# A fused attention and gated feed-forward kernel: the first half of the input weight loaded and converted in pieces of 256 columns, in a new order of the first operations

## The chip, the cores and the metric

One Trainium2 chip, one of its cores. The metric is the device time of one execution in microseconds (us), the median of the runs shown. Engines: PE (matmuls), DVE (vector), ACT (scalar), POOL (GpSimd), and SP, whose queue issues every DMA of this kernel.

## What is computed

```python
# chunked attention: 24 chunks of 32 queries, each with 16 keys to the left, 8 to the right and 8 memory keys
scores = scale * q_c @ k_full.T ; a = softmax(scores)
out[:, :, chunk] = a @ v_full            # B=4, 8 heads, 768 places, 64 wide
# gated feed-forward over x = attention output, 512 wide; moe_w_in 512x1024, moe_w_out 1024x512
h = maximum(x @ w_in, 0)
conv_out = sum over k of conv_w[k] * h shifted by k - 1 places, k = 0, 1, 2
return (h * sigmoid(conv_out)) @ w_out
```

The weights `w_in`, `conv_w` and `w_out` come in double precision, as 64-bit words; `q`, `k`, `v` and the memory are single precision.

## The kernel before

**A list of operations and an order written out by hand.** The function makes 1,818 operations; each names its engine, what it reads and what it writes. `ORDER` then says in which order they are issued. Every engine works through its own operations strictly in that order, and an operation waits until what it reads is there and until its buffer is free. The DMAs are all issued from SP's queue, in the same order.

**Attention** (`attention`, 32 steps, one for each batch, half of the sequence and pair of heads). A step n loads Q (384 KB), K (252 KB) and V (384 KB); PE makes the scores (24 small matmuls, L427, called S n here); DVE takes the row maximum (L436), ACT the exponential, DVE the row sum (L474) and its reciprocal (L476); DVE or POOL normalizes (L479); PE transposes (three matmuls, L491, T n), ACT places the result in two copies (L498); PE multiplies by V (24 small matmuls, L540, V n); ACT copies the high part of the result x (L546), and DVE makes the low part (L550). A value is held as a high and a low part, and a product of two such values is three matmuls.

**Weights** (`from_f64`). A part of `w_in` is 128 rows by 512 columns, 512 KB as 64-bit words. It is loaded into one of four `w64` buffers; ACT takes the magnitude (L306), DVE, ACT and POOL put the high and the low part together in some ten operations. The letter in `W_IN` says in which way: N (5 operations on DVE, and 4 matmuls on PE with an ACT copy behind them, L355 to L360), M (7 on DVE), S (5 on DVE, 2 on POOL), C (6 on DVE, 1 on POOL). Two `w_top` buffers hold the intermediate values, so at most two parts are in work at a time.

**Feed-forward in** (`ffn_in`). For a batch, a block fc of 128 of the 1,024 inner columns and a half hf of the sequence, PE sums over four cc (three 384-column matmuls each, L577; called a product here, fc/cc). Block fc of 0 to 3 takes columns 128 fc to 128 fc + 127 of the parts 0 to 3, one part for each cc; block fc of 4 to 7 takes the whole part fc. So before the change the first product needs all 512 columns of part 0, converted, and both parts of x from step 0; four blocks of the accumulators (`f`) are open at a time.

Then come `gated` (the convolution, the gate and the split into parts, on ACT and DVE), and the second matrix product (L793, or for batches 1 to 3 a seven-product scheme, L736).

Of the kernel before, what the change touches and what calls it, by code (L numbers as in the profile page):

```python
# [29 lines left out]
W_IN, W_OUT, W_CONV = "NMMSCMMM", "CmMMMMMC", "s"  # L30
# [193 lines left out]
def attention_then_gated_ffn(  # L224
# [68 lines left out]
    def from_f64(src, hi, lo, key, n, kind):  # L293
# [7 lines left out]
        def op(eng, cost, do, r, wr, **kw):  # L301
            plan.op(eng, cost, do, r, wr, **kw)
# [638 lines left out]
```

## Time before, and how its profile is read

| | us |
|---|---|
| median of 3 runs | 336.43 (336.32 to 336.48) |
| the profiled execution, its own time | 337.24 |
| its span, first to last instruction | 335.5 |
| PE busy in the span | 322.1 (96%) |
| DVE busy | 296.4 (88%) |
| ACT busy | 222.6 (66%) |
| POOL busy | 51.2 (15%) |

Times in the views count from the span's start. Matmuls are pipelined, so a matmul's duration covers part of the next one's; the distance from start to start says what it costs. The same holds for DVE: an instruction's duration can reach into the next.

### The profile page before, as it was taken

What the parts mean: (1) busy time and instruction counts of PE and PEld (TensorE: products, weight loads), DVE (VectorE), ACT (ScalarE), POOL (GpSimd) and SP (SyncE); (2) the same over time, 40 slices, a digit from 0 to 9 for tenths busy, and PEclk for the clock granted to TensorE, in tenths of its full rate; (3) what the DMA queues carried; (4) which work ended last, traced back from release to release, by engine and by line L of the source; (5) the groups of instructions that cost most, each with busy time, mean ns of one, the idle gap of its engine ahead of it and who ended that gap; (6) DMA issues with size and microseconds to landing.
All of it is one profiled execution on the core that took longest, in us unless ns stands there. A gap on an engine that the chain in (4) does not pass through costs nothing.

```text
span 335.5 us, 8308 instructions
## 1 busy us (share of the span) xinstructions
PE 322.1 (96%) x3259; PEld 305.1 (91%) x3259; DVE 296.4 (88%) x516; ACT 222.6 (66%) x502; POOL 51.2 (15%) x72
## 2 busy tenths in 40 slices
PE   0899999999999999999999999999999999999995
PEld 0689999999999999899988878999999999999995
DVE  3998998999999989899999999999999999599311
ACT  3588896887787879759787527658886486355210
POOL 2150310302104010410020312000000600700000
PEclk9999999999999999999999999999999999999999
DMA  8999998699697969650412545131032642011013
GB/s 278 401 372 345 388 342 291 218 300 293 202 328 230 295 193 342 218 167 34 129 61 80 195 134 198 75 146 47 2 109 64 195 135 96 26 56 63 33 65 110
DMA packets 31144, 60.87 MB, mean 181 GB/s; under 512 B 3584, under 2 KB 18048, under 8 KB 31104
## 3 DMA queue, kind: packets, MB, share of 16 engines
q1 hardware_dynamic: 31104, 60.33, 53.3%
q8 instruction: 26, 0.43, 0.5%
q14 instruction: 14, 0.11, 0.1%
HBM read 47.93 MB, written 12.39 MB: 180 GB/s over the span
## 4 chain that ended last, share of the span: by engine, by line
PE 89%; DMA 5%; DVE 2%; ACT 2%; issue 1%; SPq 0%; ACTq 0%
PE f L577 38%; PE f L736 15%; PE f L793 10%; PE s L736 7%; PE ta L540 7%; PE s L427 6%; PE ta L736 4%; DMA w<-in_w_out_dram 2%; PE ta L491 2%; DMA out_dram<-k 1%; DMA w<-in_w_in_dram 1%; ACT e L462 1%; ACT w_top L306 0%; PE f L355 0%; DVE w_top L323 0%
## 5 line engine op out<-in xcount | busy, mean ns | idle before, releaser
L577 PE MATMUL f<-u,w_in_hi 128*128 128x384 f32 x512 | 140.8, 343 | 0.6 <-ACT u L587 0.6
L577 PEld LDWEIGHTS f<-u,w_in_hi 128*128 128x128 f32 x512 | 93.2, 188 | 2.7 <-ACT u L587 1.1
L577 PE MATMUL f<-u,w_in_lo 128*128 128x384 f32 x256 | 86.0, 336 | 0.0
L607 DVE SCALAR_TENSOR_TENSOR u<-u,cw,u 128x767 f32<-128x767 f32 x64 | 64.4, 1027 | 0.1
L577 PEld LDWEIGHTS f<-u,w_in_lo 128*128 128x128 f32 x256 | 48.2, 188 | 0.2
L644 DVE TENSOR_TENSOR u<-u,u 128x768 fp32r<-128x768 f32 (+1 forms) x55 | 46.5, 871 | 0.8 <-ACT u L641 0.8
L641 ACT CAST u<-u 128x768 fp32r<-128x768 f32 (+1 forms) x56 | 41.1, 765 | 8.3 <-PE s L736 2.8
L736 PE MATMUL f<-w_in_hi,u 128*128 128x256 f32 x216 | 45.0, 282 | 0.0
L587 ACT ACTIVATE u<-f 128x384 f32<-128x384 f32 x64 | 30.6, 490 | 15.9 <-PE f L577 15.0
L736 PEld LDWEIGHTS f<-w_in_hi,u 128*128 128x128 f32 x216 | 36.0, 188 | 0.0
L616 DVE SCALAR_TENSOR_TENSOR u<-u,u 128x768 f32<-128x768 f32 x32 | 31.4, 993 | 0.4 <-ACT u L611 0.4
L793 PE MATMUL f<-w_out_hi,u 128*128 128x512 f32 x96 | 31.6, 397 | 0.0
L462 ACT ACTIVATE e<-s,top 128x64 f32<-128x64 f32 x132 | 29.3, 324 | 3.4 <-DVE w L509 1.6
L611 ACT ACTIVATE u<-u 128x768 f32<-128x768 f32 x32 | 26.8, 847 | 6.1 <-DVE u L607 6.0
L736 PE MATMUL f<-w_in_lo,u 128*128 128x256 f32 x108 | 30.3, 281 | 0.0
L598 ACT ACTIVATE u<-u,cw 128x768 f32<-128x768 f32 x30 | 28.3, 944 | 2.7 <-DVE z L476 1.3
L479 POOL TENSOR_TENSOR e<-e,z 128x384 f32<-128x384 f32 x22 | 20.6, 936 | 54.1 <-DVE z L476 35.3
L753 ACT COPY w<-f 128x256 f32<-128x256 f32 x18 | 6.6, 374 | 27.3 <-PE f L736 22.8
L427 PE MATMUL s<-k,u 128*64 128x64 f32 x672 | 24.7, 224 | 0.0
L427 PEld LDWEIGHTS s<-k,u 128*64 128x64 f32 x672 | 21.8, 138 | 3.1 <-issue 2.2
L759 DVE TENSOR_TENSOR k<-s,w 128x256 f32<-128x256 f32 x18 | 7.6, 422 | 17.1 <-PE s L736 9.6
L651 POOL TENSOR_TENSOR u<-u,u 128x384 f32<-128x384 f32 x9 | 10.8, 1200 | 74.6 <-DVE u L616 62.0
(99 smaller groups left out, 609.6 us busy)
## 6 DMA issues: line engine op xcount, KB each, us to landing
u<-in_q_dram SPq DMA_DIRECT2D x32, 384.0 KB, 6.2
u<-in_v_dram SPq DMA_DIRECT2D x25, 384.0 KB, 5.4
k<-in_k_dram SPq DMA_DIRECT2D x28, 252.0 KB, 4.9
out_dram<-k SPq DMA_DIRECT2D x36, 128.0 KB, 1.7
w<-in_w_in_dram SPq DMA_DIRECT2D x8, 512.0 KB, 6.7
w<-in_w_out_dram SPq DMA_DIRECT2D x8, 512.0 KB, 5.9
y_dram<-u SPq DMA_DIRECT2D x8, 384.0 KB, 2.8
u<-y_dram SPq DMA_DIRECT2D x8, 384.0 KB, 3.4
```

Source lines behind the costliest of these rows:

```text
L427: nc.tensor.matmul(s.t[j * D : (j + 1) * D, o : o + KW], lhsT=q_[:, c], rhs=k_t.t[:, c * STEP : c * STEP + KW], start=True, stop=True,)
L462: A.activation(keys(e)[:, g // 2, g % 2], s_()[:, g // 2, g % 2], AF.Exp, bias=top.t[:, g : g + 1], scale=SCALE)
L577: nc.tensor.matmul(f.t[:, :TW], lhsT=w_in_p[c][:, part, col : col + P], rhs=x.t[:, a * TW : (a + 1) * TW], start=(cc == 0 and i == 0), sto ...
L587: "A", act(TW, True), lambda: A.activation(h.t[:, hf * TW : (hf + 1) * TW], f.t[:, :TW], AF.Relu, scale=0.5), (f,), ((h, hf),)
L598: plan.op("A", act(S, ptr=1), lambda: A.activation(c.t, h.t, AF.Copy, scale=w[1]), H, (c,))
L607: lambda j=j, to=to, at=at: V.scalar_tensor_tensor(out=c.t[:, to], in0=h.t[:, at], scalar=w[j], in1=c.t[:, to], op0=ALU.mult, op1=ALU.add) ...
L611: plan.op("A", act(S), lambda: A.activation(c.t, c.t, AF.Tanh), (c,), (c,), table="exp")
L616: lambda: V.scalar_tensor_tensor(out=y.t, in0=c.t, scalar=1.0, in1=h.t, op0=ALU.add, op1=ALU.mult),
L641: plan.op("A", act(n), lambda: A.copy(out=hi(), in_=src()), (y,), (k_hi,))
L644: lambda: (V if eng == "V" else G).tensor_tensor(out=low(), in0=src(), in1=hi().bitcast(F32), op=ALU.subtract),
L736: nc.tensor.matmul(ps.t[:, :n], lhsT=l[a](), rhs=w[c], start=(first and j == 0 and m == 0), stop=(j == hf - 1 and m == 2), skip_group_chec ...
L793: nc.tensor.matmul(ps.t[:, :n], lhsT=gs[b, fc][a].t[:, tt * P : (tt + 1) * P], rhs=w_out_p[c][:, fc, o : o + n], start=(fc == 0 and i == 0 ...
```

## The change

The parts 0 to 3 of `w_in` are each loaded and converted in two pieces of 256 columns (called 0a, 0b, and so on), each with a key of its own, so that a product waits for its piece alone: blocks fc 0 and 1 for the a pieces, blocks 2 and 3 for the b pieces. The ways of conversion stay with the parts (0: N, 1 and 2: M, 3: S, 4: C, 5 to 7: M). That makes 40 operations more: 4 loads, 24 on DVE, 9 on ACT, 2 on POOL and 1 on PE. The order is made anew at its start: from place 306 of the old order and place 346 of the new one on, the two lists hold the same operations in the same order. The 305 and the 345 operations ahead of it are the same work, but for the split.

The PE queue at its start, before: S0, S1, S2, S3, T0, the matmuls of part 0's conversion, V0, T1, S7, 2/0, S4, V1, T3, 1/0, 3/0, 0/0, 3/1, T2, 1/1, 0/1, S6, V2, V3. After: the conversion matmuls of 0a and of 0b, S0, S1, S3, S2, T0, T1, S4, S7, V0, V1, 0/0, T2, 2/0, 3/0, 1/0, 2/1, 3/1, T3, V2, S5, V3, 0/1, 1/1, S6. In these stretches before its place 306 PE changes between attention's small matmuls and the others 18 times before and 14 times after.

The loads, before: parts 0 and 1, conv_w, K0, Q0, K1, Q1, Q2, K3, K2, Q3, part 3, Q4, V0, Q7, K7, K4, V1, part 2. After: 0a, 3a, 0b, 2a, K3, K0, Q0, 1b, K1, Q1, K2, Q2, Q7, Q3, 3b, 2b, K4, Q4, K7, V0, V1, 1a.

```diff
-W_IN, W_OUT, W_CONV = "NMMSCMMM", "CmMMMMMC", "s"
+W_IN, W_OUT, W_CONV = "NNMMMMSSCMMM", "CmMMMMMC", "s"
...
 ORDER = [
-    570, 571, 572, 573, 580, 574, 581, 582, 0, 583, 586, 12, 575, 11, 577, 587, 584, 588, 29, 585, 28, 45, 14, 15,
...
+    570, 571, 572, 573, 574, 576, 630, 575, 577, 580, 610, 578, 581, 582, 583, 584, 585, 63, 587, 12, 586, 588,
...
-            op("PE", 1396, rest, (x, (key, 0), (key, 1), (f"out{NFC - 1}", 0)), (ps,), mode="whole", late=250)
+            op("PE", 1396 * n // WC, rest, (x, (key, 0), (key, 1), (f"out{NFC - 1}", 0)), (ps,), mode="whole", late=250)
...
+    def chunk(part, col):
+
+        return f"in{2 * part + col // (WC // 2)}" if part < NFC // 2 else f"in{part + NFC // 2}"
+
+    def chunks(part):
+        return sorted({chunk(part, 0), chunk(part, WC // 2)})
...
+            key = chunk(part, col)
...
-                "PE", 520.5, mm, ((x, 0), (x, 1), (f"in{part}", 0), (f"in{part}", 1)), (f,),
+                "PE", 520.5, mm, ((x, 0), (x, 1), (key, 0), (key, 1)), (f,),
...
-    for fc in range(NFC):
-        hi, lo = (x[:, fc] for x in w_in_p)
-        from_f64(w_in[fc], hi, lo, f"in{fc}", WC, W_IN[fc])
+    for i in range(NFC // 2 + NFC):
+        part, n = (i // 2, WC // 2) if i < NFC else (i - NFC // 2, WC)
+        cols = slice(i % 2 * n, (i % 2 + 1) * n) if i < NFC else slice(0, n)
+        hi, lo = (x[:, part, cols] for x in w_in_p)
+        from_f64(w_in[part][:, cols], hi, lo, f"in{i}", n, W_IN[i])
```

In `weight_sums` and `seven`, which use the `w_in` buffers again late in the kernel, the keys of a part become the keys of its pieces.

## Rows read from the trace of the kernel before

**Rows 1.** The page: span, busy engines, chain that ended last by engine.
```profile
span 335.5 us, 8308 instructions
...
PE 322.1 (96%) x3259; PEld 305.1 (91%) x3259; DVE 296.4 (88%) x516; ACT 222.6 (66%) x502; POOL 51.2 (15%) x72
...
PE 89%; DMA 5%; DVE 2%; ACT 2%; issue 1%; SPq 0%; ACTq 0%
```

**Rows 2.** Busy time of each engine by stretch, clock, DMA share, GB/s.
```profile
0.00:20.00 20.00, 10.82 (x154) 8.86 (x154) 13.64 (x32) 10.81 (x28) 5.32 (x18) 1.00 0.94 349
20.00:54.00 34.00, 34.00 (x493) 31.37 (x490) 31.66 (x81) 27.68 (x76) 8.57 (x13) 1.00 0.98 355
...
150.00:280.00 130.00, 130.00 (x974) 122.10 (x974) 128.37 (x177) 89.19 (x156) 13.28 (x12) 1.00 0.33 108
```

**Rows 3.** Waits of PE from 54 us to the end.
```profile
PE f L577 <- ACT u L587: 0.6, 1, 0.6
```

**Rows 4.** PE in order of time: start, length, instruction, count, idle before.
```profile
7.66 3.20 PE L427 MATMUL s<-u,u 128*64 128x64 f32 x48 [7.66 <-DMA u<-in_q_dram]
11.71 1.55 PE L427 MATMUL s<-u,u 128*64 128x64 f32 x24 [0.85 <-DVE e L441]
...
20.08 0.44 PE L577 MATMUL f<-u,w_in_hi 128*128 128x384 f32 x1
...
21.55 0.87 PE L540 MATMUL ta<-a_d,u 128*64 128x64 f32 x24
22.35 0.55 PE L491 MATMUL ta<-ident,e 128*128 128x128 f32 x3
...
28.63 0.44 PE L577 MATMUL f<-u,w_in_hi 128*128 128x384 f32 x1
28.90 0.34 PE L577 MATMUL f<-u,w_in_lo 128*128 128x384 f32 x1
29.08 0.51 PE L577 MATMUL f<-u,w_in_hi 128*128 128x384 f32 x2
```

**Rows 5.** DVE in order of time.
```profile
5.12 0.43 DVE L310 TENSOR_SCALAR w_top<-w_top 128x512 f32<-128x512 f32 x1 [5.12 <-ACT w_top L306]
5.58 0.43 DVE L316 TENSOR_SCALAR w_top<-w_top 128x512 uint32<-128x512 uint32 x1
...
7.45 0.42 DVE L331 TENSOR_SCALAR w<-w 128x512 uint32<-128x512 uint32 x1
7.78 0.42 DVE L342 TENSOR_SCALAR w<-w_top 128x512 uint32<-128x512 uint32 x1
8.24 0.69 DVE L349 SCALAR_TENSOR_TENSOR w_in_lo<-w 128x512 fp32r<-128x512 uint32 x1
8.85 0.69 DVE L336 SCALAR_TENSOR_TENSOR w<-w 128x512 uint32<-128x512 uint32 x1
...
19.38 0.56 DVE L550 TENSOR_TENSOR u<-ta,u 128x384 fp32r<-128x384 f32 x1 [0.23 <-ACT u L546]
...
26.88 0.17 DVE L316 TENSOR_SCALAR w_top<-w_top 128x24 uint32<-128x24 uint32 x1
27.00 0.70 DVE L394 SCALAR_TENSOR_TENSOR w_in_lo<-w 128x512 fp32r<-128x512 uint32 x1
```

**Rows 6.** ACT in order of time.
```profile
4.43 0.66 ACT L306 ACTIVATE w_top<-w 128x512 f32<-128x512 f32 x1 [2.10 <-DMA w<-in_w_in_dram]
5.70 0.67 ACT L306 ACTIVATE w_top<-w 128x512 f32<-128x512 f32 x1 [0.62 <-DMA w<-in_w_in_dram]
...
17.45 1.34 ACT L462 ACTIVATE e<-s,top 128x64 f32<-128x64 f32 x6
...
19.86 0.96 ACT L498 COPY a_d<-ta 64x384 f32<-64x384 f32 x2
```

**Rows 7.** DMA issues at 2.58 and 11.51 us: KB, us to landing.
```profile
u<-in_q_dram SPq DMA_DIRECT2D x1, 384.0 KB, 4.9
...
u<-in_v_dram SPq DMA_DIRECT2D x1, 384.0 KB, 8.9
```

More of the change, by code (lines that the diff above doesn't have):

```diff
@@ L695, in weight_sums @@
             ws[k] = [x.rearrange("p (j n) -> p j n", n=n) for x in (hi, low)]
-            kh, kl = (tuple((f"in{2 * k + i}", p) for i in range(2)) for p in range(2))
+            kh, kl = (tuple((x, p) for i in range(2) for x in chunks(2 * k + i)) for p in range(2))
             plan.op("A", act(hf * n), lambda k=k, hi=hi: A.copy(out=hi, in_=flat(k)), (raw[k],), kh)
@@ L727, in right @@
             m = {5: 0, 6: 1, 7: 2, 4: 3}[k]
-            return [ws[m][p][:, j] for p in range(2)], tuple((f"in{2 * m + x}", p) for p in range(2) for x in range(2))
+            return [ws[m][p][:, j] for p in range(2)], tuple((y, p) for p in range(2) for x in range(2) for y in chunks(2 * m + x))
         def product(k, ps, first=False):
```

180 rows, old and new, of the table ORDER are left out of this document.

## The prediction

> **What bounds the kernel now.** I read the page first. PE is busy for 322.1 of 335.5 us and holds 89% of the chain that ended last [rows 1]. DVE comes second with 296.4 us. Busy time alone does not show a bound, because matmuls overlap, so I went on to the stretches and to PE's waits. From 20 to 54 us PE has no idle time, and none from 150 to 280 us; in this last stretch DVE is busy too, for 128.37 of 130 us [rows 2]. From 54 us to the end PE waits once, for 0.6 us [rows 3]. The matmuls also follow each other at their full pace: within a product the distance from start to start is 0.18 us (28.90 to 29.08) for a 384-column matmul [rows 4].
>
> So from about 20 us on PE works through a fixed list without a stall worth speaking of, and whatever the change is worth is decided before that. There PE has lost time: it starts at 7.66 us, when Q0 has landed, waits 0.85 us for DVE in front of S2, and the 24 small matmuls of S2 take 1.55 us where the 24 of V1 take 0.80 from start to start (21.55 to 22.35) [rows 4]. The granted clock is shown as 1.00 there [rows 2], but durations near twice the later ones are those of the lower of the two levels, 1.2 against 2.4 GHz. From 0 to 20 us the DMA engines are busy 94% of the time, and 98% up to 54 us [rows 2]: in the early stretch a load comes sooner only if another comes later.
>
> The measure is therefore: how much of its list has PE done at a given time between 20 and 54 us, after the change against before? From the 306th (346th) place on both orders are one, with no PE idle time to take up a loss and none to give back.
>
> **The change, part by part.**
>
> *DVE's added instructions.* 24 more, for the same elements. Two 512-column STT instructions start 0.61 us apart (8.24, 8.85), of which 0.53 us are 512 columns at the pace that the 24-column row fits (0.12 us from 26.88 to 27.00); a TENSOR_SCALAR of 512 costs 0.33 (7.45, 7.78), and 0.46 where the next one needs its result (5.12, 5.58) [rows 5]. So an instruction has a fixed part of 0.07 us, and 0.11 to 0.12 more in front of a dependent one. Fixed parts alone give 24 x 0.07 = 1.6 us, the lower bound; with a dependent neighbour each, 24 x 0.19 = 4.6 us, the upper one. Added up through the two orders with these prices, 48 instructions on parts 0 to 3 after and 24 before (from 5.12 to the L394 at 27.00 [rows 5]), about every second one with a dependent neighbour, they come to 14.2 us instead of 12.0: 2.2 us more. The ACT, POOL and DMA instructions that are added lie on engines that are not full (ACT 10.81 of 20 us [rows 2]), except that ACT's order counts, below.
>
> The Trainium skill speaks against the split: VectorE: DVE Perf Modes, section The TRN2 errata, gives some 150 cycles (0.156 us) as measured fixed part of an instruction and advises tiles of at least 512 elements. By it the 24 would cost 3.7 us, an estimate, instead of 2.2. The durations in the rows agree with it (0.42 us for 0.27 us of columns), the distances from start to start do not.
>
> *DVE's earlier start.* Parts 0 and 1 land at 4.4 and 5.7 us [rows 6], 1.27 us for 512 KB, so piece 0a lands 0.64 us earlier, at 3.75. ACT's L306 took 0.66 us for 512 columns; half the columns save 0.21. DVE starts at 4.2 instead of 5.12 us.
>
> *Until the first product.* Before, DVE makes x of step 0 at 19.38 [rows 5], and the product 2/0 starts at 20.08 [rows 4]. In the new order DVE has 16.4 us of instructions ahead of that: both halves of part 0 (3.4), 2a (2.1), 3a (1.6), 1b (1.8), 3b (1.5), 0.5 of 2b, and 5.5 of attention steps 0 to 3 (nine 384-column instructions of 0.47, which is 0.40 of columns and the fixed part, six small ones of 0.1, and 0.11 six times in front of a dependent one). Before, it was 14.3 us, 5.12 to 19.38, waits included. Waits: 0.3 us for ACT in front of 0b, since ACT first makes the high part of 0a; and 0.85 in front of the row sum of step 2, because its exponential is queued on ACT behind the six exponentials of step 3 (1.34 us) and the placing copies of steps 0 and 1 (0.48 each) [rows 6]. So 4.2 + 16.4 + 1.2 = 21.8, and x is there at 22.3 us.
>
> PE cannot be there much sooner either. S3 needs Q3, with which 4,208 KB have been loaded, 2,524 more than with Q0 before, which landed at 7.5 [rows 7]; at 390 KB a us, between part 1's 403 and the 349 of the stretch [rows 2, 6], that is 14.0 us. V1 needs its own load, which was issued at 11.51 and landed 8.9 later, at 20.4 [rows 7]; 232 KB more stand ahead of it now, 0.6 us, so 21.0. V1 runs from 21.15 to 21.9. SP's queue itself stops once: the load of 2b needs a buffer that POOL frees, with 3a, at about 12 us, and K4, Q4, K7 and V0 stand behind it. At that time the loads issued ahead of it still fill the DMA engines to 14.7 us, so this costs nothing; if POOL were over 2 us later, V0 would be late by the rest. The two conversion matmuls of 0a and 0b, now at the head of PE's queue, end at about 8.9; Q0 lands at 8.1 instead of 7.5, with 256 KB more ahead of it. S0 is 1.3 us later than before, but S3 has to wait for its load anyway.
>
> So the first product, 0/0, starts at 22.4. At that time PE has done S0 to S4, S7, T0, T1, V0, V1 and the conversion. Before, PE had done the same and one product more at 22.35 [rows 4]. That is 0.55 us behind.
>
> *From there to place 346.* I followed PE's queue against DVE, ACT and the loads with the durations of the rows. Most suppliers come in time, by 0.2 to 2 us (the last converted piece, 2b, at 30.4 against the product 2/2 at 31.0). One does not: V3 is queued behind S5 and needs two placing copies, which on ACT stand behind step 4's exponentials and 1a's high part; they end at 28.1 and PE is there at 27.75. Cost 0.4 us. On the other side PE changes 14 times between small matmuls and others, before 18 times. After such a change the first of a product's matmuls is followed at 0.27 instead of 0.18 us [rows 4], so 4 x 0.1 = 0.4 us are saved.
>
> **The sum.** 0.55 + 0.4 - 0.4 = 0.5 us later at place 346, and at the end. The profiled execution took 337.24 us (span 335.5 and 1.7 around it), 0.8 above the median of 336.43. 337.24 + 0.5 = 337.7 for such an execution, **336.9 us** for the median. Less than 0.2% (0.67 us) cannot be told from no change here.
>
> **The rivals.**
>
> *DVE is held up by its added instructions, slower.* If each costs 0.19 us instead of 0.09 on the average, 17 of the 24, those ahead of x of step 0, make it 1.7 us later: the first product at 24.1, all else behind it. 336.9 + 1.7 = 338.6. With half of that, 337.8. For it: DVE is busy nearly throughout, PE's suppliers have little in hand, and every stall counts in full. Against it: the distances in [rows 5]. It decides once DVE is 0.6 us later than my sum at piece 2b, because then 2/2 waits as well. By the fixed part that the Trainium skill states (VectorE: DVE Perf Modes, The TRN2 errata) the first product would be 1.1 us later than in my sum, and the time 338.0, an estimate.
>
> *DVE and ACT gain, faster.* If the added instructions cost the lower bound (0.6 us less than I count) and the two waits of 1.2 us do not come, x of step 0 is there at 20.6, V3's copies are in time, and V1, if its load lands at the pace of 390 KB a us (4,692 KB behind Q0's 7.5, at 19.5), is done by 20.6 as well. Then the first product starts 1.2 us earlier, and V3's 0.4 is not lost: 336.9 - 1.6 = 335.3. For it: pieces let fc 0 begin with half of part 0, and the new order opens with less idle time. Against it: the DMA engines are full, and Q3 and V0 stand deeper in the queue than before. It decides when V1 ends before 21.4.
>
> *The later order swallows it.* PE's one wait of 0.6 us [rows 3] could take up the 0.5 us, if what it waits for does not shift: 336.4. Against it: ACT's result waited for there comes from PE's own products, which shift along.
>
> **How the numbers follow.** My forecast, a small loss, gets 0.50, with a range of its own of 335.9 to 337.5: of it 0.36 within 0.2% (335.76 to 337.10), 0.13 slower, 0.01 faster. DVE held up: 0.24, slower. DVE and ACT gain: 0.20, faster. Swallowed: 0.06, the same. Together faster 0.21, same 0.42, slower 0.37. The range leaves out what lies beyond the faster rival's 335.3 and the upper part of the slower one: 335.2 to 338.3.
>
> **What would show it.** PE's first product at 22.4 us with S4, S7 and V1 ahead of it; 21.9 or earlier speaks for a gain, 23.5 for the slower rival. DVE's first instruction at 4.2; x of step 0 at 21.8; the 24-column distance kept, 256 columns at 0.20 (TENSOR_SCALAR) and 0.33 (STT). A wait of PE or a gap in front of V3 of about 0.4. No PE wait between 32 and 140 us. After 54 us every PE instruction should be later by one same amount; if this amount changes between 54 and 280 us, DVE has become the bound there, and the forecast is wrong in its main point.

## The result, and the profile after

| | before | after |
|---|---|---|
| median | 336.43 (335.68 to 336.7, 5 runs) | 339.18 (338.81 to 339.96, 5 runs) |
| ratio | | 1.007 (1.0042 to 1.0097) |
| profiled execution, span | 337.24, 335.5 | 339.70, 337.8 |

The change makes the kernel some 2.4 us slower by the ratio, 0.7%; the two medians lie 2.75 us apart. The forecast was 336.9, its range ended at 338.3. Below, "shift" is by how much an instruction of PE is later than the same one in the profiled execution of before; "place 346" is where the two orders become one.

The page of the changed kernel, to be held against [rows 1]. PE's share of the chain that ended last has fallen from 89 to 84%, ACT's has risen from 2 to 5%.

```profile
span 337.8 us, 8369 instructions
...
PE 323.6 (96%) x3263; PEld 307.1 (91%) x3263; DVE 299.9 (89%) x540; ACT 223.5 (66%) x511; POOL 51.0 (15%) x74
...
PE 84%; DMA 6%; ACT 5%; DVE 1%; issue 1%; POOL 0%; SPq 0%; ACTq 0%; DVEq 0%
```

Busy time by stretch of the changed kernel, with the columns of [rows 2], and then one stretch of the kernel before.

```profile
8.00:18.00 10.00, 6.88 (x94) 6.17 (x96) 9.08 (x30) 4.92 (x16) 1.95 (x3) 1.00 1.01 364
18.00:30.00 12.00, 11.29 (x196) 10.06 (x195) 11.64 (x34) 11.19 (x36) 4.36 (x7) 1.00 1.03 394
...
20.00:56.00 36.00, 35.29 (x534) 32.67 (x533) 34.33 (x91) 29.47 (x84) 9.62 (x15) 1.00 0.89 328
150.00:280.00 130.00, 130.00 (x969) 122.09 (x968) 128.39 (x177) 88.25 (x154) 12.79 (x12) 1.00 0.34 111
```
```profile
8.00:18.00 10.00, 8.49 (x104) 6.72 (x103) 9.09 (x23) 5.99 (x18) 1.83 (x3) 1.00 1.04 402
18.00:30.00 12.00, 12.00 (x206) 11.02 (x207) 10.71 (x25) 10.19 (x31) 4.87 (x5) 1.00 1.02 357
```

From 8 to 30 us PE is busy for 18.17 us after and 20.49 before, 2.32 us less. That is not the loss itself: before 8 us PE has been busy 1.28 us longer than before the change (1.62 and 0.34), with the conversion matmuls of 0a; those of 0a and 0b take 3.2 us in all, where part 0's took 1.9. From 8 to 18 us DVE is as busy as before (9.08 and 9.09). ACT does 1.07 us less in that stretch and then has hardly a gap (11.19 of 12). After 54 us PE shows no wait, and its shift stays nearly the same to the end: 2.2 us at place 346, 2.5 at 137 us, and 2.0 from 142 us on, since before's own wait of 0.6 us at 140.85 [rows 3] falls away there.

PE in order of time in the changed kernel, to be held against [rows 4].

```profile
9.58 1.55 PE L429 MATMUL s<-u,u 128*64 128x64 f32 x24
12.18 1.55 PE L429 MATMUL s<-u,u 128*64 128x64 f32 x24 [1.05 <-DMA u<-in_q_dram]
15.79 2.83 PE L429 MATMUL s<-u,u 128*64 128x64 f32 x48 [2.06 <-DMA u<-in_q_dram]
18.55 1.33 PE L493 MATMUL ta<-ident,e 128*128 128x128 f32 x6
19.82 1.79 PE L429 MATMUL s<-k,u 128*64 128x64 f32 x48
21.43 0.87 PE L542 MATMUL ta<-a_d,u 128*64 128x64 f32 x24
22.52 0.92 PE L542 MATMUL ta<-a_d,u 128*64 128x64 f32 x24 [0.22 <-ACT a_d L500]
23.37 0.44 PE L587 MATMUL f<-u,w_in_hi 128*128 128x384 f32 x1
...
29.68 0.92 PE L542 MATMUL ta<-a_d,u 128*64 128x64 f32 x24 [0.47 <-ACT a_d L500]
```

S1 waits 1.05 us for Q1 and S3 2.06 for Q3: 3.1 us in front of two loads, where the kernel before waited 1.5 us in all between 8 and 18 us (0.85 of it in [rows 4]). The first product is at 23.37; before, PE had the same work done at some 21.65 (22.35, less 0.7 for the product 2/0). It is 1.7 us behind, where I had reckoned 0.55.

The 1.7 us add up in PE's own queue. S3 starts 1.97 us later than before (15.79 and 13.82), when Q3 has landed at 15.66; from there to the first product PE has 0.45 us less to do, S2 in place of the conversion; and it waits 0.22 us for ACT in front of V1. PE's pace is not what differs: S0 to S3 take 1.4 to 1.6 us each in both profiles. Two more suppliers are as late: V1's load lands at 22.35, and ACT's copy for V1 ends at 22.47. Q2 had landed at 13.68, and DVE was done with step 0's scores by 13.3. So as far as the trace shows, S2, which the new order puts behind S3, could have run while PE waited for Q3. No run tried that.

The chain of waits, followed back from V3, says what the time went through there: first the changed kernel, then the kernel before. The wait for Q3 lies beside it.

```profile
6.66 5.38 DMA u<-in_q_dram
...
12.18 1.57 PE s L429 x24
...
15.04 1.34 ACT e L464 x6
...
18.40 1.11 ACT e L464 x5
...
19.76 0.48 ACT a_d L500
20.26 0.41 ACT w_in_hi L381
20.69 0.85 ACT a_d L500 x2
...
22.49 0.48 ACT u L548
...
26.63 1.35 ACT e L464 x6
28.01 0.21 ACT e L473
28.24 0.41 ACT w_in_hi L330
28.67 0.47 ACT a_d L500
29.16 0.48 ACT a_d L500
...
29.68 0.92 PE ta L542 x24
```
```profile
12.42 1.35 ACT e L462 x6
...
13.82 1.55 PE s L427 x24
15.36 0.83 PE ta L491 x3
16.20 1.32 PE f L355 x2
17.52 0.45 PE f L357 x2
17.97 0.85 PE ta L540 x24
```

Before, PE sets its own pace from S3 at 13.82 us on. After, the chain runs over Q1's load and S1, then for the most part over ACT until V3 at 29.68: step 1's six exponentials, step 3's, then the placing copies of step 0 with the copy of a piece between them, the high part of x, step 4's exponentials, the copy of 1a, the copies of step 3. Before, ACT makes step 0's placing copies ahead of step 3's exponentials, while PE is busy with the conversion matmuls (L355, L357):

```profile
16.29 0.96 ACT L498 COPY a_d<-ta 64x384 f32<-64x384 f32 x2 [0.66 <-PE ta L491]
```

DVE after, to be held against [rows 5]: start, length, and the waits.

```profile
3.92 0.29 DVE L312 TENSOR_SCALAR w_top<-w_top 128x256 f32<-128x256 f32 x1 [3.92 <-ACT w_top L308]
4.24 0.29 DVE L318 TENSOR_SCALAR w_top<-w_top 128x256 uint32<-128x256 uint32 x1
4.57 0.43 DVE L325 SCALAR_TENSOR_TENSOR w_top<-w,w_top 128x256 uint32<-128x256 uint32 x1
5.03 0.29 DVE L344 TENSOR_SCALAR w<-w_top 128x256 uint32<-128x256 uint32 x1
...
6.86 0.29 DVE L312 TENSOR_SCALAR w_top<-w_top 128x256 f32<-128x256 f32 x1 [1.07 <-ACT w_top L308]
...
13.77 0.56 DVE L438 TENSOR_REDUCE top<-s 128x6 f32<-128x384 f32 x1 [0.47 <-PE s L429]
...
23.04 0.52 DVE L552 TENSOR_TENSOR u<-ta,u 128x384 fp32r<-128x384 f32 x1
```

And the DMA packets of the first 16 us, after and before: 4.86 MB against 5.40.

```profile
DMA packets 2310, 4.86 MB, mean 303 GB/s; under 512 B 251, under 2 KB 789, under 8 KB 2310
```
```profile
DMA packets 2159, 5.40 MB, mean 337 GB/s; under 512 B 358, under 2 KB 882, under 8 KB 2159
```

### The profile page after: what moved, and what is told of

It reads as the page before. It is cut to its first block, busy times and chain, and to the rows that moved or that the text cites. A ratio compares the mean times of both kernels' runs of the same rounds, so it can differ in the third digit from the quotient of the medians.

```text
span 337.8 us, 8369 instructions
## 1 busy us (share of the span) xinstructions
PE 323.6 (96%) x3263; PEld 307.1 (91%) x3263; DVE 299.9 (89%) x540; ACT 223.5 (66%) x511; POOL 51.0 (15%) x74
## 4 chain that ended last, share of the span: by engine, by line
PE 84%; DMA 6%; ACT 5%; DVE 1%; issue 1%; POOL 0%; SPq 0%; ACTq 0%; DVEq 0%
PE f L587 37%; PE f L746 14%; PE f L803 10%; PE s L746 7%; PE ta L542 6%; PE s L429 6%; PE ta L746 4%; DMA w<-in_w_out_dram 2%; DMA out_dram<-k 2%; DMA u<-in_q_dram 2%; ACT e L464 1%; PE ta L493 1%; ACT a_d L500 1%; DMA w<-in_w_in_dram 1%; ACT w_top L308 0%
## 5 line engine op out<-in xcount | busy, mean ns | idle before, releaser
L617 DVE SCALAR_TENSOR_TENSOR u<-u,cw,u 128x767 f32<-128x767 f32 x64 | 63.7, 1017 | 0.1
L542 PE MATMUL ta<-a_d,u 128*64 128x64 f32 x600 | 21.5, 224 | 0.7 <-ACT a_d L500 0.7
```

Source lines behind the costliest of these rows:

```text
L542: nc.tensor.matmul(y, lhsT=v_g[:, g, u, h], rhs=a_d.t[:, :, o], start=(by_v or g + u == 0), stop=True, skip_group_check=not by_v,)
L617: lambda j=j, to=to, at=at: V.scalar_tensor_tensor(out=c.t[:, to], in0=h.t[:, at], scalar=w[j], in1=c.t[:, to], op0=ALU.mult, op1=ALU.add) ...
```

## Experiments

Operations stand by their numbers in the order. Times are medians, with the ratio to the kernel before on the same chip and its interval; "first product" and the shift at place 346 are from the profiled execution. For profiled executions of the old order that shift was -0.3 to -0.4 in three runs (e1, e4, k3 below), so the profile of before is itself that much late, and the changed kernel's 2.2 is some 2.5 against these. But a profiled execution is one sample: in h3, the old order too, the shift was +1.9, and the profiled execution was the fastest of its run in e1, g1, g3, g4 and k1 and the slowest in h2 and h3. The intervals of the runs in the new order, g4's apart, overlap the changed kernel's own, so what these runs gain or lose against it, up to 1.1 us, is no more than a hint.

**The parts of the change alone, in the old order (two runs), and two repairs of the new order (two runs).**

```diff
+        if key in ("in0", "in1", "in2", "in3"):
+            def halves():
+                for h in range(2):
+                    c = slice(h * n // 2, (h + 1) * n // 2)
+                    nc.sync.dma_start(out=w.t[:, c].rearrange("p n w -> p (n w)"), in_=src[:, c].bitcast(U32))
```
Run e1: the kernel before, loads of parts 0 to 3 in halves.

> The kernel before, with each load of parts 0 to 3 issued as two DMAs of 256 columns (rows of 2 KB instead of 4 KB), one behind the other; order and conversions as they were. Load theory, with the loss in the form of the loads: parts 0 and 1 land 1 us later or more (before 4.4 and 5.7), V1's load follows (before 20.4, then 21.4 or later), time +0.6 to +1.5 us against before. If the form does not matter (the loss lies in what stands ahead, in SP's stops, or in chance): part 1 lands within 0.5 us of 5.7, V1's load within 0.3 of 20.4, time within 0.5 us. DVE theory: no change.

336.99, ratio 1.0021 (0.9997 to 1.0044). The first megabyte lands at 6.8 us instead of 5.7, S0 starts at 8.79 instead of 7.66 and S3 at 14.70 instead of 13.82; the first product is at 19.72, not later than before (20.08). Part of that is PE's pace: S2 and S3 took 0.92 us each in this execution, 1.55 before. In h3 below the loads are as late and S3 starts at 14.64, but its 24 matmuls take 1.55 us and the first product is at 22.00. First e1, then h3:

```profile
14.70 0.92 PE L435 MATMUL s<-u,u 128*64 128x64 f32 x24 [0.86 <-ACT e L470]
```
```profile
14.64 1.55 PE L435 MATMUL s<-u,u 128*64 128x64 f32 x24 [0.46 <-ACT e L470]
```

```diff
+            def halves():
+                for h in (slice(0, n // 2), slice(n // 2, n)) if two else (slice(0, n),):
+                    now[0] = h
+                    do()
+            plan.op(eng, cost, halves, r, wr, **kw)
```
Run e4: the kernel before, conversion instructions of parts 0 to 3 in halves.

> The kernel before, same loads and same order, with each instruction of the conversion of parts 0 to 3 issued as two of 256 columns: 24 more on DVE, 9 on ACT, 2 on POOL, 4 matmuls more on PE. DVE theory: 16 of the 24 come before the first product, at 0.07 to 0.19 us each 1.1 to 3 us; the first product (20.08) and the time later by 1.1 to 3 us against before. Load theory (in the changed kernel DVE waited for loads and hid its added work): here DVE has little idle time ahead of the first product, so up to +1.1 us; under +0.4 us if other waits hide it.

336.5, ratio 1.0006 (0.9985 to 1.0028). All added DVE, ACT and POOL instructions together cost nothing that can be measured in the old order, and 0.9 us at most by the interval.

```diff
-        w = Tile("w64")
+        small = n == WC // 2
+        w = Tile("u", dtype=U32) if small else Tile("w64")
```
Run e2: the changed kernel, pieces in other buffers.

> The changed kernel, with the eight pieces loaded into buffers of the large pool u instead of the four w64 buffers, so that SP never stops for one (it stopped from 3.5 to 5.8 us in front of 1b, and from 9.4 to 13.1 in front of 2b). Load theory, with the loss in SP's stops: V1's load lands 0.5 to 1.3 us earlier than 22.35, the first product (23.37) is earlier by as much, time -0.4 to -1.3 us against the changed kernel. If SP's stops cost nothing, as the prediction had it: V1's load and the time within 0.3 us. DVE theory: no change.

338.88, ratio 1.0075 (1.0048 to 1.0103). SP no longer stops, but Q1 and Q3 land within 0.1 us of where they did: SP's stops (two, where I had reckoned one) cost nothing, as I had said.

```diff
-    595, 75, 74
+    75, 74, 595
```
Run e3: the changed kernel, ACT's copy of 1a (595) behind two placing copies of step 3.

> The changed kernel, with ACT's copy of the high part of piece 1a moved behind the two placing copies of step 3, for which V3 waited 0.5 us on PE. If that wait is part of the loss, as the prediction had it: V3 0.4 us earlier, everything behind it too, time -0.4 us. If the wait only moves on (another supplier is as late): V3 earlier, place 346 not, time unchanged.

338.62, ratio 1.0065 (1.0042 to 1.0088). V3 follows without a gap, as meant; but V1's load landed 0.9 us later in this execution (first product at 24.19), and V3 starts at 29.67, where it did: what was saved in front of V3 had been lost in front of V1.

**Is it the loads, or DVE?**

```diff
-610, 63, 12, 11
+610, 47, 63, 12, 11
```
(SP's queue; 47 is V2's load.)
Run g1: the changed kernel, V2's load first.

> The changed kernel, with the load of V2 (384 KB) moved ahead of K3's, so that all loads from K3 to V1 come behind 384 KB more; nothing else is moved. Theory A (the first loads land 1.3 to 1.7 us later than I reckoned, and three chains that begin at a load, Q1's, Q3's and V1's, set the first product together): 384 KB at some 390 KB a us make each of these loads 1.0 us later, the first product comes at 24.3 instead of 23.4, and the time grows by 0.9 to 1.1 us against the changed kernel, to 340.1. Theory B (DVE is held up by its added instructions and the loads wait for nobody): under 0.3 us, 339.3.

339.92, ratio 1.0083 (1.0067 to 1.0100). First product at 24.18, 0.8 later; shift at place 346 2.7, 0.5 more; in the time some 0.4 more. Q3 came 0.6 us later, not 1.0, since the three loads behind Q0 took 2.33 us this time instead of 2.75. In this execution later loads cost about their lateness at place 346, as in theory A; in the medians the 0.4 us are within the intervals, so theory B is not excluded by the time.

```diff
-            lambda: on.tensor_scalar(out=ftop(), in0=ftop(), scalar1=TINY, scalar2=None, op0=ALU.max), (x,), (x,), shared=True,
+            lambda: n == WC // 2
+            or on.tensor_scalar(out=ftop(), in0=ftop(), scalar1=TINY, scalar2=None, op0=ALU.max), (x,), (x,), shared=True,
```
Run g2: the changed kernel, eight DVE instructions left out.

> The changed kernel, with the DVE instruction that puts a lower bound under the magnitudes left out for the eight pieces: eight instructions of 256 columns less, some 0.3 us each, five of them ahead of x of step 0. This part of the computation is left out. Theory A: V1's load and Q3's bind within 0.2 us of DVE's chain, so the time stays within 0.3 us of the changed kernel's 339.2. Theory B: 1.4 us less work for DVE ahead of x of step 0 brings the first product forward by as much, 337.8.

338.23, ratio 1.0044 (1.0025 to 1.0063); shift at place 346 1.6. It gains 0.9 us against the changed kernel, between the theories. The control is the same in the old order:

Run k3:

> The kernel before, with the same DVE instruction left out for the parts 0 to 3 (four instructions of 512 columns, 0.33 to 0.46 us each; this part of the computation is not done). In the changed order leaving it out gave 0.9 us. If DVE is short of time only in the new order, the time stays at that of the kernel before within 0.4 us; if DVE holds PE up in the old order too, it falls by 0.6 us or more.

336.5, ratio 0.9977 (0.9956 to 0.9998): 0.8 us there too. Within intervals of 0.7 us to either side, less work on DVE is worth the same in both orders: nothing here says that DVE is shorter of time in the new one.

**Reliefs of the loads, alone and together.** The loads' order, and S4 (82) behind T2 (56):

```diff
-570, 630, 580, 610, 63, 12, 11, 600, 29, 28, 46, 45, 130, 62, 640, 620, 80, 79, 131, 13, 30, 590
+570, 580, 630, 610, 12, 11, 600, 29, 28, 46, 45, 63, 62, 640, 620, 130, 131, 13, 30, 80, 79, 590
```
Run g3:

> The changed kernel with loads in another order: 0b ahead of 3a, K3 directly ahead of Q3, Q7 behind 2b, K4 and Q4 behind V1; S4 then stands behind T2 in PE's queue. Q1 comes 0.65 us sooner, Q3 1.0, V0 and V1 1.6. If one load alone were the cause (theory C: Q3's or V1's), the first product would come 1.0 to 1.6 us sooner. By theory A the chain from Q1's load through DVE's softmax and ACT's copies takes its place and gives 0.6 us; S4 has to be made up behind, so the time stays between 338.6 and 339.2. Theory C: 337.7.

339.55, ratio 1.0069 (1.0051 to 1.0087). The first product comes at 22.73, 0.6 sooner, as theory A says, but S4 is then still to be done; shift at place 346 1.8. The time is 0.35 us above theory A's range.

Run h2, with the diffs of g2, g3 and e3:

> The changed kernel with three reliefs at once: the lower bound of the pieces left out (this part of the computation is not done), the loads in the order of the run with relieved loads (with S4 behind T2), and ACT's 1a copy behind the two placing copies that V3 needs. Alone they gave some 0.9, 0.1 and 0.2 us. If the chains run side by side and end nearly together, so that one hides what another gives, together they give more than the sum of 1.2: the time comes to 337.0 to 337.7. If each gives its own and no more, 338.0.

338.57, ratio 1.0068 (1.0050 to 1.0086), shift 1.8: less than the sum, and my expectation of more was wrong. Q1 and Q3 came 0.4 and 0.7 us sooner, and V0 and V1 wait 0.51 and 0.38 us for ACT's copies.

Run k1, with the diffs of g3, e2 and e3:

> The changed kernel with the loads in the order of the run with relieved loads (0b ahead of 3a, K3 directly ahead of Q3, Q7 behind 2b, K4 and Q4 behind V1, S4 behind T2), with the pieces in other buffers so that SP never stops in front of a load, and with ACT's 1a copy behind the two placing copies of step 3. With the stop, the relieved order brought Q1 only 0.1 us and Q3 0.45 us sooner; without it they should come 0.7 and 1.0 us sooner than in the changed kernel. Theory A (PE's idle time in front of S1 and S3, 3.1 us, is what the change costs; later loads cost about their lateness, as V2's load showed): S3 starts at 14.7, the shift at place 346 falls from 2.2 to 1.2 to 1.4, and the time to 338.0 to 338.4. Theory B (DVE's queue holds the softmax of steps 0 and 1 whenever the loads come): the idle time moves to the front of V0 and T2, the shift stays at 1.8 to 2.0, the time at 338.7 to 339.2.

339.4, ratio 1.0071 (1.0049 to 1.0094). S3 starts at 14.61, 1.2 us sooner, and the shift falls to 1.5; in the medians nothing of it is seen (the profiled execution is the lowest). S7, V0 and V1 now wait 0.43, 0.50 and 0.38 us for ACT:

```profile
18.80 0.92 PE L427 MATMUL s<-k,u 128*64 128x64 f32 x24 [0.43 <-ACT e L462]
20.23 0.92 PE L540 MATMUL ta<-a_d,u 128*64 128x64 f32 x24 [0.50 <-ACT a_d L498]
21.53 0.92 PE L540 MATMUL ta<-a_d,u 128*64 128x64 f32 x24 [0.38 <-ACT a_d L498]
```

Together 1.31 us: what the loads gave, ACT's queue took. Here, as in h2 and k2, ACT's queue is seen to hold PE up in the new order.

Run k2, with the diffs of k1 and g2:

> The run before this one, and the lower bound of the pieces left out as well (this part of the computation is not done): eight DVE instructions less. Theory A: 0.2 to 0.3 us less than that run, since DVE is not what PE waits for. Theory B: 0.7 us or more less. If both hold PE up in turn, this is the run in which the shift at place 346 falls below 1.0 us and the time to 337.6 or less.

338.33, ratio 1.0036 (1.0016 to 1.0056), shift 1.1. That is 1.1 us less than k1, nearer theory B's 0.7 or more than theory A's 0.2 to 0.3, so with the loads relieved DVE may count too; the shift did not fall below 1.0, nor the time to 337.6, which I had expected if both held PE up in turn. With every relief that I had, the new order is still 1.2 us slower than the old one without any, and some 2.0 us slower than k3 (0.9977), in which the same DVE work is left out.

**Two misses.** The first 345 places rearranged, the pieces as they are:

```diff
-    570, 571, 572, 573, 574, 576, 630, 575, 577, 580, 610, 578, 581, 582, 583, 584, 585, 63, 587, 12, 586, 588,
+    570, 571, 12, 580, 610, 11, 572, 573, 574, 581, 576, 575, 577, 578, 582, 583, 584, 616, 14, 611, 617, 585, 612,
...
```
Run g4:

> The changed kernel, pieces and conversions as they are, with the first 345 places put in another order: found by moving operations within their engine's queue in a replay that uses the durations of the changed kernel's trace and lets loads land at 330 KB a us at first. In the replay the 420th place is 1.2 to 1.8 us sooner than in the changed order. If the order of the start is what costs the time, and not the pieces, the time falls by that much, to 337.4 to 338.0. If the pieces themselves cost it, it stays at 339 or above.

341.71, ratio 1.0143 (1.0124 to 1.0162): worse. PE waits 2.0 us for a reciprocal of DVE and 1.95 for POOL, which the replay had not seen, and behind these waits the granted clock is 0.50 from 18 to 24 us. It does not tell pieces from order; it tells that replayed durations don't hold when neighbours change.

```diff
+        if i < NFC:
+            src = src[i % 2 * (P // 2) : (i % 2 + 1) * (P // 2)].rearrange("r (t n) -> (r t) n", t=2)
```
Run h1, in the changed kernel:

> The changed kernel, with the parts 0 to 3 of w_in laid out in memory so that a piece is one block of 256 KB; the loads, their sizes and the 2 KB that each of 128 partitions gets stay the same. In the changed kernel the first four pieces (1 MB) have landed at 7.0 us, in the kernel before the first two parts (1 MB) at 5.7. If reading every other 2 KB of memory is what makes the pieces slow, they land at 5.7 here, everything behind them 1.2 us sooner, and by what 1.0 us of lateness cost with V2's load first (0.8 us at the first product, 0.4 in the time) the time falls by 0.5 to 1.0 us against the changed kernel, to 338.2 to 338.7. If it is the number of loads or the 2 KB, they land at 7.0 and the time stays at 339.2.

Run h3, the same in e1:

> The kernel before with the parts 0 to 3 loaded in two halves, as in the run with loads in halves, but laid out in memory so that a half is one block. There the first four halves (1 MB) had landed at 6.8 us, against 5.7 with whole parts, and the time was the same. If reading every other 2 KB is what makes halves slow, they land at 5.7 here; if it is the number of loads or the 2 KB per partition, at 6.8. The time is that of the kernel before in either case, within 0.5 us.

The first megabyte lands at 6.9 and 6.7 us: reading every other 2 KB is not what makes the pieces slow. Times 338.88, ratio 1.0075 (1.0041 to 1.0108), and 337.64, ratio 1.0028 (1.0006 to 1.0050). For h3 that is 0.9 us above the kernel before, where I had expected 0.5 at most, and its interval leaves out 1: halves do cost something in the old order.

**The order itself: two of its moves, in the kernel before.** ACT's placing copies of step 0 (24, 23) behind step 3's exponentials (67, 68):

```diff
-24, 23, 67, 68, 26
+67, 68, 24, 23, 26
```
Run k5:

> The kernel before, with one thing of the new order: ACT's two placing copies of step 0 stand behind step 3's six exponentials instead of ahead of them. In the kernel before they run at 16.29 and 16.77 us and the exponentials from 17.45 to 18.79; in the changed one the copies run at 19.76 and 20.69, behind the exponentials. Theory D (the new order makes x of step 0 wait for step 3, whose load comes last of the first four): the copies end at 19.4, V0 starts at 19.4 instead of 17.9, the first product comes 1.5 to 2.0 us later, and the time grows by 1.0 to 2.0 us. If the queue on ACT matters little, since PE has S7 and T1 to do meanwhile, under 0.5 us.

337.13, ratio 1.0015 (1.0000 to 1.0031), shift 0.4. V0 waits only 0.22 us: the exponentials move forward, and the conversion matmuls keep PE busy meanwhile. 0.5 us, the lower expectation; the granted clock is 0.55 to 0.60 from 14 to 18 us.

The conversion matmuls of part 0 (578) ahead of S2 (48) on PE, with ACT's copy for them (576) ahead of part 1's (585):

```diff
-14, 31, 48, 65, 22, 578, 25
+14, 31, 578, 48, 65, 22, 25
```
Run k6:

> The kernel before, with the other thing that the new order does on PE: the conversion matmuls of part 0 (1.9 us, at 15.99 between T0 and V0) stand ahead of S2, where PE waits 0.85 us, and ACT's copy for them ahead of that of part 1. In the changed kernel they run ahead of S0, in idle time. If PE's list from S3 on is what counts, 1.0 us or more is gained at V0 and the time falls by 0.5 to 1.0; if V0 then waits for ACT's copies (they end at 17.25) and S2 and S3 come later, under 0.5 us either way.

337.51, ratio 1.0030 (1.0012 to 1.0048), shift 1.4. PE now waits 2.11 us in front of V0, for the copies, and the granted clock in the 6 us behind that is 0.72. Neither expectation: 1.0 us lost. (In this execution Q0 landed at 8.81 instead of 7.53, so part of the shift is the loads'.)

Run k7, both diffs:

> The kernel before with both moves of the two runs before this one: the conversion matmuls ahead of S2, and ACT's two placing copies of step 0 behind step 3's exponentials. Alone they cost some 1.0 and 0.5 us. If the conversion matmuls covered the copies (PE worked on them while ACT copied), the copies' lateness counts in full once the cover is gone: V0, at 17.9 in the run with the conversion matmuls early, starts at 19.0 or later, and the two together cost 2.0 us or more, 338.8 to 339.3, about what the whole change costs. If they simply add up, 1.5 us, 338.3; if one hides the other, 1.0 us, 337.8.

339.69, ratio 1.0079 (1.0049 to 1.0109), shift 2.9. PE in order of time, and the stretch from 18 to 24 us with its granted clock, of this kernel, and then V0 in the kernel before:

```profile
14.67 0.55 PE L487 MATMUL ta<-ident,e 128*128 128x128 f32 x3
18.17 1.55 PE L536 MATMUL ta<-a_d,u 128*64 128x64 f32 x24 [2.95 <-ACT a_d L494]
19.65 0.90 PE L487 MATMUL ta<-ident,e 128*128 128x128 f32 x3
...
21.96 0.69 PE L573 MATMUL f<-u,w_in_hi 128*128 128x384 f32 x1
```
```profile
18.00:24.00 6.00, 5.83 (x68) 4.83 (x70) 3.68 (x9) 2.55 (x6) 2.98 (x3) 0.50 1.00 353
```
```profile
17.90 0.92 PE L540 MATMUL ta<-a_d,u 128*64 128x64 f32 x24
```

V0 starts at 18.17 (expected: 19.0 or later), behind an idle time of 2.95 us, and then PE runs at 0.50, the 1.2 GHz level, for 6 us: V0 takes 1.48 us from start to start, where it took 0.85 before. Apart the moves cost 0.5 and 1.0 us, together 2.7 (336.57 x 0.0079), as much as the whole change, with whole parts and whole loads. That each covered the other is likely, but the 1.2 us above the sum are no more than the intervals allow. And the time goes another way than in the changed kernel: V0 starts only 0.27 us later than before (18.17 and 17.90), and the rest comes behind it, at the lower clock. The profile of the changed kernel shows a granted clock of 1.00 from 8 to 56 us and no such idle time in front of V0.

## Why the prediction was wrong

The step that failed is the first term of the sum: the first product, at 22.4 with PE 0.55 us behind. It was at 23.37, 1.7 behind, because each of the chains that I had followed to it was longer than I had reckoned, and ACT's I had not followed through. 0.2 us of the difference are my price of 0.5 us for the product 2/0, which takes 0.7 (20.08 to 20.80). The other terms held roughly: V3's wait 0.47 us (0.4 said); some 0.3 us regained between 32 and 40 us (0.4 said, for fewer changes of kind; by the traces there are 22 of them up to place 346, and 26 before, four fewer as I had counted). 1.7 + 0.5 - 0.3 = 1.9; where the other 0.3 of the 2.2 measured at place 346 arose was not found. That PE's list decides and that a loss there goes through to the end was right, and the one late wait took up some 0.5 us of it, which I had given a chance of 0.06 as the whole story.

Inside the first product, with the loads as what PE itself waited for longest:

- *ACT's order.* I had followed DVE to x of step 0 and let ACT come in with one wait of 0.85 us. But in the new order x of step 0 hangs on ACT behind step 3: placing copies behind its exponentials, these behind S3, S3 behind Q3's load. I had the words for it in the list of V3's wait, and did not apply them to V0. DVE made the low part of x at 23.04, 0.07 us after ACT had made the high one; I had said 21.8. In the changed kernel PE lost 0.22 us by ACT ahead of the first product, in k1, with the loads sooner, 1.31 us: ACT's chain was the next one behind the loads'.
- *The cover.* I booked the conversion matmuls at the head of the queue as hidden in idle time. True, but in the old place they were what PE did while ACT copied. k6 and k7 show that the old order leaves PE idle for 2.1 and 2.95 us without that cover; the changed kernel shows no such idle time, so what the cover is worth there is not shown.
- *The loads.* I took 390 KB a us, and put the four added loads at nothing, as lying on an engine that is not full, though my own rows show the DMA engines busy for 94% of the first 20 us. (Ahead of Q0 stand 228 KB more, not 256.) The first four pieces landed at 7.0 us where 1 MB in whole parts landed at 5.7; S3 started at 15.79 (14.1 by my 14.0), and V1's load landed at 22.35 (21.0). With that V1 could not have ended before 23.2, whatever ACT and DVE did. Of Q3's 1.7 us of lateness 1.2 were there at Q0 (9.30, 8.1 said). In the old order the same lateness cost 0.7 and 0.9 us in the time (e1, h3; the first not clear of noise), in the new one, in one profiled execution, most of it (g1). My reading that S0 may be late since S3 waits for its load anyway overlooked that S1, and with it the whole chain, waits for Q1.
- *DVE.* Its first instruction at 3.92 (4.2), distances of 0.32 us in front of a dependent instruction and 0.46 for an STT as reckoned, waits of 1.5 us instead of 1.2, and not the two that I had named: 1.07 in front of 0b, whose load landed at 6.37, and 0.47 for S1. But the instructions ahead of x took 17.6 us from start to start, not 16.4: two of them took 0.6 us where their like took 0.2 to 0.35 (L396 at 18.04, L344 at 21.00). So DVE had no idle time left either in front of 23.04. The slower rival had the sign, 338.6; that its cause, a price of 0.19 us for each added instruction, is at work is not shown: in the old order they cost 0.9 us at most (e4), and less DVE work is worth about the same in both (g2, k3). The Trainium skill, VectorE: DVE Perf Modes, section The TRN2 errata, which advises tiles of 512 elements and more, had spoken against the split; no run here shows a cost of the smaller tiles that can be measured.

What is shown, and what not. Shown: in the old order more conversion instructions cost nothing measurable, and half loads cost 0.7 and 0.9 us in two runs, the second clear of noise; in the new order PE loses its time in front of Q1's and Q3's loads, and loads that come 1.2 us sooner give only a part of it back, since ACT's queue is as late (k1, one profiled execution). The two moves alone, without any split, cost as much as the change, but by a fall of the clock that the changed kernel does not show. Argued only: that these two moves are also what costs the time inside the new order. There PE's idle time stands in front of S1 and S3 and not in front of V0, and the moves were not taken back in it: S7 needs the score buffer that step 3's exponentials free, so the copies can't simply go ahead of them. So the cause of the 2.4 us as a whole stays open: loads, ACT's order and DVE's queue end within 0.5 us of each other at the first product. Why 1 MB in pieces lands 1 us later stays open as well; the layout in memory is excluded, the number of loads and the 2 KB per partition were not told apart. The DMA engines were not left idle for it: from 3 to 5 us they were busy 90% of the time at 288 GB/s with pieces, and 100% at 390 with whole parts. No version beat the kernel before, but for the one that leaves work out.

## What to carry to other kernels

Before an order is judged by the engine that is busiest, follow the first result through every queue, and ask of each instruction ahead of it whether it belongs to a later step: here copies behind another step's exponentials tied the first product to the fourth load. Work moved from a busy stretch into idle time is a gain only if nothing was hidden behind it in its old place. When several chains end within 0.5 us of each other, relieving one shows little; put the suspected moves into the old kernel instead, singly and together, and then see whether the time goes there by the same way: here the sum was as large, but it went by the clock.

## What the runs showed of the hardware

- After PE had been idle for 2.95 us (k7) the granted clock was 0.50 for 6 us although PE was busy, and the score matmuls of a step took 1.48 us instead of 0.85; after 2.11 us (k6) it was 0.72 over 6 us. V0, T1, S7, 2/0 and S4 took 6.3 us together (18.17 to 24.46), before 3.65 [rows 4]: the slow stretch cost 2.6 us beside the idle time. The clock fell in k5, g3, g4 and k2 too (0.50 to 0.60 over stretches of 4 to 6 us), each time after PE had run 24 score matmuls in 0.92 us and had then waited, once or more, 0.9 to 2.4 us.
- A granted clock of 1.00 in the first 20 us does not say that PE is at its upper level: S3 and S2 together take 2.83 us in the changed kernel at 1.00, and the same 2.83 us in g3 and k2 at 0.50. In one order the pace changed at different times: at about 13 us in e1 and at about 20 us in h3, both with 1.00 shown, and the first product was at 19.72 and 22.00.
- 1 MB of 64-bit words in four loads of 256 KB landed at 6.6 to 7.4 us in the runs with pieces or halves, in two loads of 512 KB at 5.6 to 5.8.
- In the kernel before a 16 KB packet of instructions began at 17.71 us and took 1.1 us; V1's load, under way then, landed 2.4 us behind the load ahead of it (18.05 and 20.45), where 384 KB otherwise took 1.0. That the one causes the other was not tested.
